# Five experts' rows of x gathered as quarter rows and turned by VectorE in 32x32 blocks instead of by TensorE

## The chip, the cores and the metric

One core of one Trainium2 chip runs one program. Its engines are TensorE (PE in the profile, its weight loads PEld), VectorE (DVE), ScalarE (ACT), GpSimd (POOL) and SyncE (SP), which work from queues of their own, in order, and wait for each other by semaphores. The metric is the device time of one execution in microseconds (us); lower is better.

## The reference

Attention over 8 batches of 448 tokens with 12 heads of 64, then a mixture of 8 experts over the 3584 rows of its output. The routing is greedy: all 3584 x 8 logits are sorted, and a token goes to its best expert that still has room, 448 rows each.

```python
x = attention(q, k, v, cap)                 # [3584, 768]; scores are cap * tanh(scores / cap)
logits = x @ w_gate                         # [3584, 8]
for idx in np.argsort(-logits.flatten()):   # greedy, 448 rows to an expert
    ...
for e in range(8):
    mask = assigned == e
    h = np.maximum(x[mask] @ w1[e], 0.0)    # w1[e] is [768, 1024]
    out[mask] = h @ w2[e]                   # w2[e] is [1024, 768]
```

## The kernel before

**Stages.** Attention takes the first 340 us or so and leaves x in DRAM (`xs`, one row of 768 floats to a token). Then the routing's first round runs, and from about 390 us `ffn_all` goes through the experts in the order in which the routing fills them, p = 0 to 7. All products are made to nearly full fp32 precision out of two halves: every operand is split into a high part (ScalarE copies it to fp32r: `xgh`, `w1h`, `w2h`) and the rest (`xgl`, `w1l`, `w2l`: the operand minus its high part). VectorE makes the rests of x, GpSimd those of the weights (line 723, called by `split1` and `split2`).

**One expert.** `ffn1` makes h in 8 blocks f of 128 columns, each of 18 matmuls (6 chunks c of the 768 inputs, three products each): 144 matmuls. `ffn2` makes the output in 8 units u (two column halves, four tiles of rows), 24 or 16 matmuls each: 176. Every matmul calls `tick`, and these 320 ticks per expert are the clock by which everything else is put between them when the program is written: engines marked for manual scheduling (TensorE, ScalarE, VectorE, GpSimd) run in exactly the order written.

**x of the next expert.** When the routing has the row numbers of expert p+1, `tick` calls `gather` (line 746): four indirect DMAs from GpSimd's queue fetch 128, 128, 128 and 64 rows of 3 KB into the one buffer `xg`, token on the partition. In units u = 5, 6 and 7 of `ffn2` of expert p, `xtr` (line 762) turns chunk after chunk: four TensorE transpositions into a PSUM tile `psX`, a ScalarE copy to `xgh` (line 767) and a VectorE subtraction to `xgl` (line 768). The list `CP` says after which matmul of which unit a chunk comes: one in u = 5, three in u = 6, two in u = 7. The first layer's weights are loaded so that chunk c holds input rows 128c to 128c+127 (line 707).

**The routing.** `phases0` is a generator that `tick` resumes; each `yield n` says after how many ticks it goes on, a negative number at which tick of all. For p = 1 to 7 it proposes each token's best expert, searches the threshold in three selects of four steps each (on VectorE five compares, line 484, and a step that reads a TensorE sum, lines 488 to 496), and takes the winner (`best`, with `qq` of line 559 and `sx` of line 548 on VectorE). Then `finalise` makes the row numbers: VectorE writes two masks and a running count (lines 573 to 577); 12 ticks later TensorE sums the counts over partitions (line 584); VectorE makes positions and two one-hot tables (lines 588 to 602); 18 ticks later TensorE multiplies them (line 606); and after two more small steps `idx` is there (line 617). The winner of p is searched while expert p-1 is computed. The line `yield -((p-1)*320+145)` holds `finalise` back until tick 145 of expert p-1, which is the second matmul of its `ffn2`. Counted in ticks of expert p-1, the search for p ends at 101 (p = 3), 100 (p = 4, 5, 6); the last expert needs none.

**GpSimd's queue** in an expert: 14 or so splits of weights, one about every nine ticks through `ffn1`, with a one-element memset between two (`gap`), the last at tick 137 (w2's second half, piece 3); then the gather; then in `ffn2` four scattered writes of the expert before (line 804) and the first two splits for the next expert.

Of the kernel before, what the change touches and what calls it, by code (L numbers as in the profile page):

```python
# [6 lines left out]
F32=mybir.dt.float32; F32R=mybir.dt.float32r; BF16=mybir.dt.bfloat16; F16=mybir.dt.float16; I32=mybir.dt.int32; I16=mybir.dt.int16  # L7
AF=mybir.ActivationFunctionType; ALU=mybir.AluOpType; AX=mybir.AxisListType
# [9 lines left out]
def attention(nc, tc, c1, xp, pM, q, k, v, cap, w_gate, xs, L1, ident, on_logits, on_turn, NDEF, xd, setup):  # L18
# [3 lines left out]
    B,H,S,D=q.shape  # L22
    CP=112; NJ=S//CP; NP=H//2; NQ=NP//2; E=w_gate.shape[1]; HG=2
    N=B*NQ
    xT={}; rin={}; xn={}; spilled={}; todo=list(range(B-NDEF,B-2))
    def xt(b,p,late=None):
# [5 lines left out]
        if p==0:  # L32
            alt=late and (b in spilled and (b-B)%2 or b==B-1)
            xn[b]=(late[1] if alt else xp).tile([CP,NJ,H,D],F32,name="xn",bufs=1)
        ps=late[0].tile([128,512],F32,name="psL") if late else pM.tile([128,512],F32,name="psM")
        for j in range(NJ):
            nc.tensor.transpose(ps[:CP,j*128:(j+1)*128],xT[b][:,p,j*CP:(j+1)*CP],ident)  # L37
        def rest():
            src=ps[:CP,:].rearrange("p (j h d) -> p j h d",j=NJ,h=2)
            if late:  # L40
                raw=late[1].tile([CP,512],F32,name="raw")
                nc.scalar.activation(raw,ps[:CP,:],AF.Copy)  # L42
                src=raw.rearrange("p (j h d) -> p j h d",j=NJ,h=2)
# [264 lines left out]
ACF=1  # L308
LF=1
TA=0  # L310
EW=1; WT=4; PB=lambda nc: nc.gpsimd
FMAX=3.4028234e38
class Routing:
    def __init__(s, nc, cp, NT, E):
# [3 lines left out]
    def setup(s):  # L318
        nc=s.nc; cp=s.cp; E=s.E; NT=s.NT
        CP=112; NC=s.NC  # L320
        t=lambda n,sh,dt=F32: cp.tile(sh,dt,name="r_"+n)
# [39 lines left out]
        nc.vector.tensor_scalar(qi,qi,4,None,op0=ALU.arith_shift_right)  # L361
        s.qm=t("qm",[128,32])
        nc.gpsimd.tensor_scalar(s.qm,qi,8.0,None,op0=ALU.is_equal)
        kv=t("kv",[128,3])
        nc.gpsimd.iota(kv,[[1,3]],base=1,channel_multiplier=0,allow_small_or_imprecise_dtypes=True)
        G=16*(NC//16)*112
# [3 lines left out]
        for n,base,f in (("A",1.0,2.0),("B",-2048.0,2.0**-12),("C",1024.0,2.0**-22)):  # L370
            S=s.steps[n]
            T0=s.T0[n]=t("T0"+n,[128,3]); H=s.H[n]=t("H"+n,[128,S,6]); C=s.C[n]=t("C"+n,[128,S,3])
            x=float(4**(S-1))
# [128 lines left out]
    def search(s,wp,turned=()):  # L502
# [66 lines left out]
    def finalise(s,wp,L,update):  # L569
        nc=s.nc; T=s.T; NC=s.NC; v=nc.vector  # L570
# [11 lines left out]
        ps=s.psum()  # L582
# [21 lines left out]
        ps=s.psum()  # L604
# [7 lines left out]
        ps=s.psum()  # L612
        s.selmm=nc.tensor.matmul(ps[:,:28],s.sel,ev,start=True,stop=True)
        v.scalar_tensor_tensor(s.ixf[:,:28],ps[:,:28],float(s.NT//2),s.qm[:,:28],op0=ALU.add,op1=ALU.mult)
        idx=wp.tile([128,4],I32,name="idx",bufs=8)
        with nc.allow_low_precision(reason="one term of each sum is not zero"):
            mark=v.tensor_reduce(idx,s.ixf.rearrange("p (t r) -> p t r",r=8),axis=AX.X,op=ALU.add)
        s.results.append((idx,s.ei))
        yield 1
        if update:  # L620
          with s.tc.issue_after(mark.ins) if s.cur==0 else nullcontext():
            z=wp.tile([112,1],F32,name="zz")
# [15 lines left out]
    def phases0(s,wp,L,turned):  # L638
        HA=[7,10]; HB=3
        for p in range(s.E):  # L640
            s.hA=HA[min(p,len(HA))-1] if p else 7; s.hB=HB; s.na=2 if p<9 else 1
            s.cur=p
            if p:
                s.propose(L,0,s.NC)
                yield 30
            yield from (s.search(wp,turned if p==0 else ()) if p<s.E-1 else s.last(wp))
            yield -((p-1)*320+145) if p>1 else 4
            yield from s.finalise(wp,L,p<s.E-1)


# [1 line left out]
def ffn_all(nc, tc, ctx, rt, xs, w1, w2, out, ident, E, wp, deferred, xctx, gen):  # L652
    C=448; DM=768; DC=6; DF=1024; FC=8; HD=384
# [3 lines left out]
    res=rt.results  # L657
# [34 lines left out]
    f2=ctx.enter_context(tc.tile_pool(name="f2",bufs=1))  # L692
# [9 lines left out]
    def load1(p,i,gate=None):  # L702
        if p>=E: return
        e=expert(p)
        t=ws.tile([128,DC,128],F32,name="w1r",bufs=W1B)
        if gate is not None: nc.gpsimd.tensor_copy(t[0:1,0,0:1],gate)
        nc.sync.dma_start(t,w1[bass.ds(e,1),:,i*128:i*128+128].rearrange("o (c p) f -> p (o c) f",p=128))
        raw[p,1,i]=t
    def load2(p,i,gate=None):
        if p>=E: return  # L710
# [21 lines left out]
        view=use=lambda t:t.rearrange("p (o d) -> p o d",o=2)  # L732
        cut((p,2,hf,i),src,[128,2*HD],"w2",8,None,view,use)
    xgs={}; xgT={}
    CP=[[int(y) for y in x] for x in ',,,,,0,123,45'.split(',')]
    CL=[[[]]*6+[[None,0,1],[2,3]],[[]]*6+[[0,1,2],[3,4]]]
    def newx(p):
        if p not in xgT: xgT[p]=(fp.tile([128,DC,C],F32R,name="xgh"),fp.tile([128,DC,C],F32R,name="xgl"))
# [2 lines left out]
    def gather(p):  # L741
        if p>=E or p in xgs: return
        need(p)
        t=xgs[p]=xgp
        for j,(o,n) in enumerate(TS):
            g=nc.gpsimd.indirect_dma_start(out=t[:n,j*DM:(j+1)*DM],out_offset=None,in_=xs,in_offset=bass.IndirectOffsetOnAxis(ap=res[p][0][:n,j:j+1],axis=0))
        return g
    def tx(p,n):
        newx(p)
        w=rt.psum()  # L750
        ps=[(ph.tile([128,512],F32,name="psH") if c>1 else pt.tile([128,512],F32,name="psX")) for c in range(n)]
        for j,(o,_) in enumerate(TS):
            for c in range(n): nc.tensor.transpose(ps[c][:,o:o+128],xgs[p][:,j*DM+c*128:j*DM+c*128+128],ident)
            if j<len(TS)-1: warm(WJ,w)
        for c in range(n): cutx(p,c,ps[c])
    def xtr(p,c):
        if p>=E or c is None: return
        newx(p)
        gather(p)
        ps=pt.tile([128,512],F32,name="psX")  # L760
        for j,(o,n) in enumerate(TS):
            nc.tensor.transpose(ps[:,o:o+128],xgs[p][:,j*DM+c*128:j*DM+c*128+128],ident)  # L762
        cutx(p,c,ps)
    def cutx(p,c,ps):
        h,l=xgT[p]
# [44 lines left out]
    def ffn2(p,t,hf,cs,work={}):  # L810
        if p not in ons: ons[p]=(f2.tile([128,3*DM],F32,name="on"),f2.tile([64,DM],F32,name="on3"))
        ps=ph.tile([128,512],F32,name="psH")
        h=hh[p]
        o,n=TS[t]
        terms=((o,0),(512+o,0),(o,1)) if t<3 else ((o,0),(o,1))
        m=0; nm=FC*len(terms)
        for f in range(FC):
            for a,w in terms:
                nc.tensor.matmul(ps[:,:HD],h[:,f,a:a+128],spl[p,2,hf,f//2][w][:,f%2,:],start=(m==0),stop=(m==nm-1))  # L819
                m+=1  # L820
                tick()
                if m%8==4 and m//8<len(cs): xtr(p+1,cs[m//8])
                for z in work.get(m,()): z()
        cols=slice(hf*HD,hf*HD+HD)
        if t<3: nc.scalar.activation(ons[p][0][:,t*DM+hf*HD:t*DM+hf*HD+HD],ps[:,:HD],AF.Copy)  # L825
        else:
            y=f2.tile([64,HD],F32,name="y3",bufs=2)
            nc.scalar.activation(y,ps[64:128,:HD],AF.Copy)
            nc.vector.tensor_tensor(ons[p][1][:,cols],ps[:64,:HD],y,op=ALU.add)
# [17 lines left out]
    for p in range(E):  # L847
        lastp=p==E-1; cur[0]=p
        for f in range(FC):
            if f==0: load2(p,2)  # L850
            if f+W1B-1<FC and (p==0 or f+W1B-1>=W1B): load1(p,f+W1B-1) if (p,1,f+W1B-1) not in raw else None
            if f==2: load2(p,3)
            work={}
            if f+2<FC and (p,1,f+2) not in spl: work[3]=[lambda: split1(p,f+2)]
            at={0:[(11,0,0)],1:[(11,0,1)],2:[(11,0,2)],3:[(11,1,0)],4:[(11,0,3)],5:[(11,1,1)],6:[(11,1,2)],7:[(11,1,3)]}
            if p==0: at={1:[(11,0,0)],2:[(11,0,1)],3:[(11,0,2)],4:[(11,0,3)],5:[(11,1,0)],6:[(3,1,1),(11,1,2)],7:[(3,1,3)]}
            for n,hf,i in at.get(f,()): work[n]=[lambda hf=hf,i=i: split2(p,hf,i)]
            if p==1 and f==0: work[1]=[lambda: xtr(1,5)]
# [12 lines left out]
        for u in range(8):  # L871
            if u==4: load1(p+1,0); load1(p+1,1)
            if u==5: load1(p+1,2); load2(p+1,0)
            if u==6: load1(p+1,3)
            if u==7: load2(p+1,1)
            wk={5:{14:[lambda: split1(p+1,0)]},6:{8:[lambda: split1(p+1,1)]}}.get(u,{})
            if p<1 and u==7: wk={15:[lambda: xtr(p+1,4+p)]}
            ffn2(p,u%4,u//4,(CL[p] if p<1 else CP)[u],wk)
            if u>3: pend.append((p,u%4))


# [58 lines left out]
```

## Time and profile before

| | us |
|---|---|
| median of 3 runs | 919.64 |
| lowest, highest | 918.25, 920.63 |
| the profiled execution | 920.52 |
| its span, first to last instruction | 918.8 |
| experts' stage in the trace | from about 390 to 911 |
| one expert's `ffn1` and `ffn2`, p = 4 | 657.1 to 687.9 and 687.9 to 723.1 |

The profile gives for each engine its busy time, groups of instructions by line with count, busy time and mean, and the idle time before them with what ended it. `f32 x8` after shapes is a count. The timeline has one line per instruction: start, length, engine, line, operation, output<-inputs; in square brackets the idle time before it. Matmuls are pipelined, so the step from one start to the next is what a matmul costs, not its length. Row "PE psH L791 x16" of the chain in order of time means sixteen matmuls of the first layer in the time shown.

### The profile page before, as it was taken

What the parts mean: (1) busy time and instruction counts of PE and PEld (TensorE: products, weight loads), DVE (VectorE), ACT (ScalarE), POOL (GpSimd) and SP (SyncE); (2) the same over time, 40 slices, a digit from 0 to 9 for tenths busy, and PEclk for the clock granted to TensorE, in tenths of its full rate; (3) what the DMA queues carried; (4) which work ended last, traced back from release to release, by engine and by line L of the source; (5) the groups of instructions that cost most, each with busy time, mean ns of one, the idle gap of its engine ahead of it and who ended that gap; (6) DMA issues with size and microseconds to landing.
All of it is one profiled execution on the core that took longest, in us unless ns stands there. A gap on an engine that the chain in (4) does not pass through costs nothing.

```text
span 918.8 us, 17575 instructions
## 1 busy us (share of the span) xinstructions
PE 880.7 (96%) x6318; PEld 640.7 (70%) x6318; DVE 611.0 (67%) x2012; ACT 582.2 (63%) x836; POOL 351.9 (38%) x514
## 2 busy tenths in 40 slices
PE   7899999999999997799999999999999999999996
PEld 4333444444333335688989989989989899999996
DVE  3777988989788688776777776766777764231210
ACT  6999999999999957273482662662752742522520
POOL 7200000000000008583494392492682673754831
PEclk9999999999999999799999999999999999999999
DMA  8799999997993007750914516416406407426201
GB/s 119 115 132 131 137 166 170 134 159 134 192 142 88 1 5 256 233 205 27 322 47 162 196 40 228 137 33 232 147 18 249 147 2 264 131 72 246 78 10 52
DMA packets 291704, 123.09 MB, mean 134 GB/s; under 512 B 224768, under 2 KB 275712, under 8 KB 291104
## 3 DMA queue, kind: packets, MB, share of 16 engines
q1 hardware_dynamic: 285104, 99.70, 48.0%
q0 software_dynamic: 4656, 22.02, 6.4%
q8 instruction: 50, 0.82, 0.4%
q10 hardware_dynamic: 1856, 0.23, 0.2%
q14 instruction: 38, 0.31, 0.1%
HBM read 97.15 MB, written 24.77 MB: 133 GB/s over the span
## 4 chain that ended last, share of the span: by engine, by line
PE 73%; ACT 9%; issue 9%; DVE 4%; POOL 3%; DMA 1%; SPq 0%; POOLq 0%; ACTq 0%; DVEq 0%
PE psH L791 22%; PE psH L819 22%; PE psA L187 10%; PE psS L149 8%; ACT e L155 5%; PE psM L204 3%; ACT e L159 3%; PE psS L154 2%; PE psX L762 2%; DVE cmpD L484 1%; POOL out_dram L804 1%; POOL w1l L723 1%; PE psL L37 1%; POOL w2l L723 1%; PE psM L215 1%
## 5 line engine op out<-in xcount | busy, mean ns | idle before, releaser
L819 PE MATMUL psH<-w2h,hh 128*128 128x384 f32 x896 | 249.0, 343 | 0.0
L819 PE MATMUL psH<-w2l,hh 128*128 128x384 f32 x512 | 174.5, 341 | 0.0
L155 ACT ACTIVATE e<-psS,s 128x896 f32<-128x896 f32 x168 | 160.7, 995 | 19.3 <-PE psS L149 11.4
L819 PEld LDWEIGHTS psH<-w2h,hh 128*128 128x128 f32 x896 | 162.7, 189 | 0.2
L159 ACT ACTIVATE e<-e,bias,capt 128x1792 f32<-128x1792 f32 (+2 forms) x74 | 154.2, 2084 | 2.5
L791 PE MATMUL psH<-xgh,w1h 128*128 128x448 f32 x384 | 142.9, 372 | 0.3 <-ACT xgh L767 0.3
L45 POOL TENSOR_TENSOR xn<-raw,rin 112x512 f32<-112x512 f32 x24 | 24.4, 1049 | 309.9 <-ACT raw L42 308.7
L149 PE MATMUL psS<-tq,tk 64*64 64x448 f32 x1152 | 130.5, 546 | 12.4 <-ACT e L155 12.4
L791 PE MATMUL psH<-xgl,w1h 128*128 128x448 f32 x384 | 141.9, 370 | 0.0
L791 PE MATMUL psH<-xgh,w1l 128*128 128x448 f32 x384 | 141.2, 368 | 0.0
L723 POOL TENSOR_TENSOR w2l<-w2r,w2h 128x768 fp32r<-128x768 f32 x64 | 118.1, 1846 | 11.0 <-ACT w2h L719 10.8
L723 POOL TENSOR_TENSOR w1l<-w1r,w1h 128x768 fp32r<-128x768 f32 x62 | 114.3, 1843 | 20.7 <-ACT w1h L719 16.8
L187 PE MATMUL psA<-e,nv 64*64 64x448 f32 x1104 | 122.0, 547 | 0.2 <-ACT e L159 0.2
L825 ACT ACTIVATE on<-psH 128x384 f32<-128x384 f32 x48 | 23.6, 492 | 127.3 <-PE psH L819 122.1
L163 DVE TENSOR_TENSOR es<-es,e 64x896 f32<-64x896 f32 (+2 forms) x74 | 100.5, 1359 | 4.8 <-ACT e L159 3.5
L799 DVE SCALAR_TENSOR_TENSOR hh<-psH,hh 128x64 fp32r<-128x64 f32 (+1 forms) x128 | 44.0, 386 | 85.2 <-ACT hh L797 84.6
L149 PEld LDWEIGHTS psS<-tq,tk 64*64 64x64 f32 x1152 | 41.9, 132 | 80.7 <-ACT e L155 45.7
L819 PEld LDWEIGHTS psH<-w2l,hh 128*128 128x128 f32 x512 | 96.6, 189 | 0.0
L187 PEld LDWEIGHTS psA<-e,nv 64*64 64x64 f32 x1104 | 44.8, 134 | 62.1 <-issue 50.5
L797 ACT ACTIVATE hh<-psH 128x448 fp32r<-128x448 f32 x64 | 34.7, 542 | 70.5 <-PE psH L791 66.3
L791 PEld LDWEIGHTS psH<-xgh,w1h 128*128 128x128 f32 x384 | 72.5, 189 | 6.1 <-ACT xgh L767 0.5
L791 PEld LDWEIGHTS psH<-xgh,w1l 128*128 128x128 f32 x384 | 72.3, 188 | 5.6
(317 smaller groups left out, 1305.3 us busy)
## 6 DMA issues: line engine op xcount, KB each, us to landing
w1r<-in_moe_w_dram SPq DMA_DIRECT2D x64, 384.0 KB, 4.2
w2r<-in_moe_w_dram SPq DMA_DIRECT2D x32, 768.0 KB, 7.8
k<-in_k_dram SPq DMA_DIRECT2D x92, 112.0 KB, 3.3
q<-in_q_dram SPq DMA_DIRECT2D x92, 112.0 KB, 3.9
nv<-in_v_dram SPq DMA_DIRECT2D x72, 128.0 KB, 3.9
xs<-xn SPq DMA_DIRECT2D x4, 1344.0 KB, 7.6
xs<-xn SPq DMA_DIRECT2D x4, 896.0 KB
xd<-xT SPq DMA_DIRECT2D x2, 1344.0 KB
```

The lines of the kernel that those rows point to most:

```text
L45: (nc.gpsimd if late else nc.vector).tensor_tensor(xn[b][:,:,h0:h0+3:2,:],src, rin[b][:,:,2*p:2*p+2].unsqueeze(3).broadcast_to([CP,NJ,2,D] ...
L149: for c in range(2): nc.tensor.matmul(ps[c*64:c*64+64,h,:S],tks[g,0][hp,o,u*128+c*64:u*128+c*64+64],tks[g,1][hp,o,:],start=True,stop=True)
L155: nc.scalar.activation(ev(g,r),ps[:,:,:S],AF.Tanh,scale=s1)
L159: nc.scalar.activation(e,e,AF.Exp,scale=capt,bias=bias)
L163: t=es_t[g]; add=lambda o,a,b: nc.vector.tensor_tensor(o,a,b,op=ALU.add)
L187: nc.tensor.matmul(avp[g,o][h*64:h*64+64,:S],lhs,rhs[hp,h,:],start=(j==0 and x==0),stop=(j==3 and (g<N-1 or o==0)))
L204: nc.tensor.matmul(ps[g*32:g*32+32,:S],lhs,rhs,start=first,stop=last)
L723: (eng or nc.gpsimd).tensor_tensor(view(l),r,view(h).bitcast(F32),op=ALU.subtract)
L791: nc.tensor.matmul(ps[:,:C],a[:,c,:],b[:,c,:],start=(m==0),stop=(m==DC*3-1)); m+=1
L797: nc.scalar.activation(h[:,:C],ps[:,:C],AF.Relu)
L799: nc.vector.scalar_tensor_tensor(h[:,d:d+b-a],ps[:,a:b],0.0,h[:,a:b].bitcast(F32),op0=ALU.max,op1=ALU.subtract)
L819: nc.tensor.matmul(ps[:,:HD],h[:,f,a:a+128],spl[p,2,hf,f//2][w][:,f%2,:],start=(m==0),stop=(m==nm-1))
```

## The change

For the experts p = 3 to 7 (`GN=3`):

- `finalise` makes a second table `idg` [128, 14] of row numbers for quarter rows (a 32-partition block b holds quarter b of 32 tokens), with two more VectorE instructions; `setup` makes two constants for it.
- `gather` issues fourteen indirect DMAs of 128 quarter rows (768 bytes each) instead of four of whole rows.
- `turnx` takes the place of the four transpositions: one VectorE transposition of 32x32 blocks per chunk reads every sixth float of `xg` and writes `xt` in SBUF; ScalarE makes `xgh` and VectorE `xgl` from `xt`, the subtraction of a chunk written behind the transposition of the next. Each call puts the routing's next step off by five ticks.
- One chunk moves from u = 5's first place to its third; the other five keep their places.
- `finalise` is held only until tick 90 of expert p-1 (for p = 7 the number is 60, and the six times five ticks bring it to 90).

For all experts the first layer's input rows are taken in another order: chunk c holds rows 6i + c on partition i. So w1 is loaded in that order, and the transpositions that stay with TensorE (p = 0, 1, 2) read every sixth float of `xg` as their weights.

```diff
-EW=1; WT=4; PB=lambda nc: nc.gpsimd
+EW=1; GN=3; WT=4; PB=lambda nc: nc.gpsimd
...
-        s.results.append((idx,s.ei))
+        idg=None
+        if s.cur>=GN:
+            gx=wp.tile([128,28],F32,name="gx",bufs=1)
+            v.scalar_tensor_tensor(gx,ps[:,:28],s.gb,s.gm,op0=ALU.add,op1=ALU.mult)
+            idg=wp.tile([128,14],I32,name="idg",bufs=2)
...
+                v.tensor_reduce(idg,gx.rearrange("p (t r) -> p t r",r=2),axis=AX.X,op=ALU.add)
+        s.results.append((idx,s.ei,idg))
...
-            yield -((p-1)*320+145) if p>1 else 4
+            yield -((p-1)*320+(90 if p<7 else 60)) if p>1 else 4
...
-        nc.sync.dma_start(t,w1[bass.ds(e,1),:,i*128:i*128+128].rearrange("o (c p) f -> p (o c) f",p=128))
+        nc.sync.dma_start(t,w1[bass.ds(e,1),:,i*128:i*128+128].rearrange("o (p c) f -> p (o c) f",c=DC))
...
+    CN=[[[int(y) if y!='-' else None for y in x] for x in z.split(',')] for z in (',,,,,--0,123,45',)*2]
...
+        if p>=GN:
+            for j in range(14):
+                nc.gpsimd.indirect_dma_start(out=t[:,j*192:j*192+192],out_offset=None,in_=xs.rearrange("n (b d) -> (n b) d",b=4),in_offset=bass.IndirectOffsetOnAxis(ap=res[p][2][:,j:j+1],axis=0))
+            return
...
+    def chunk(p,j,c): return xgs[p][:,j*DM:j*DM+DM].rearrange("t (d c) -> t d c",c=DC)[:,:,c]
+    half=[]
+    def turnx(p,c):
+        x=f2.tile([128,C],F32,name="xt",bufs=2)
+        nc.vector.transpose(x.rearrange("p (t i) -> p t i",i=32),xgs[p][:,:14*192].rearrange("p (t d c) -> p t d c",d=32,c=DC)[:,:,:,c])
+        h,l=xgT[p]
+        nc.scalar.activation(h[:,c,:],x,AF.Copy)
+        half.append(lambda: nc.vector.tensor_tensor(l[:,c,:],x,h[:,c,:].bitcast(F32),op=ALU.subtract))
+        cnt[0]-=5
+        while len(half)>(1 if c<DC-1 else 0): half.pop(0)()
...
+        if p>=GN: return turnx(p,c)
...
-            nc.tensor.transpose(ps[:,o:o+128],xgs[p][:,j*DM+c*128:j*DM+c*128+128],ident)
+            nc.tensor.transpose(ps[:,o:o+128],chunk(p,j,c),ident)
...
-            ffn2(p,u%4,u//4,(CL[p] if p<1 else CP)[u],wk)
+            ffn2(p,u%4,u//4,(CL[p] if p<1 else CP if p+1<GN else CN[p>3])[u],wk)
```

**Where instructions move.** TensorE, the counts' sum of `finalise` for p = 5: before, it stands among the second layer's matmuls (`w2h`, `w2l`) of expert 4.

```order
L819 MATMUL psH<-w2l,hh 128x384
L819 MATMUL psH<-w2h,hh 128x384
L584 LDWEIGHTS r_lo
L584 MATMUL psR<-scan,r_lo 112x2
L585 LDWEIGHTS r_up
L585 MATMUL psR<-scan,r_up 112x1
L819 MATMUL psH<-w2h,hh 128x384
```

In the changed kernel it stands among the first layer's (`xgh` or `xgl` with `w1h` or `w1l`), behind matmul 102 of the 144.

```order
L823 MATMUL psH<-xgl,w1h 128x448
L823 MATMUL psH<-xgh,w1l 128x448
L593 LDWEIGHTS r_lo
L593 MATMUL psR<-scan,r_lo 112x2
L594 LDWEIGHTS r_up
L594 MATMUL psR<-scan,r_up 112x1
L823 MATMUL psH<-xgh,w1h 128x448
```

TensorE's sum, and with it everything behind it, now follows VectorE's count 50 matmuls earlier, in `ffn1`. On VectorE the same `finalise` stood behind six `hh` instructions (the last three blocks of h) that separated it from the end of the search; now it follows `sx` directly.

```order
L568 SCALAR_TENSOR_TENSOR qq<-r_K_340,wA,r_K_341 112x32
L552 TENSOR_TENSOR wt<-psR,wm 112x8
L554 TENSOR_REDUCE wB<-wt 112x1
L557 SCALAR_TENSOR_TENSOR sx,e8s<-wt,wB,r_e8c 112x8
L582 TENSOR_SCALAR gt<-qq,wB 112x32
L583 TENSOR_SCALAR gteq<-qq,wB 112x32
L584 SCALAR_TENSOR_TENSOR gteq<-r_kk,e8s,gt 112x32
L586 SCALAR_TENSOR_TENSOR scan<-r_ones_174,gteq 112x64
```

The three `hh` pairs that came between `sx` and `gt` have moved: one behind `scan`, one behind `oi`, one behind `ev`. GpSimd's queue at the gather for p = 5, in the changed kernel:

```order
L739 TENSOR_TENSOR w2l<-w2r,w2h 128x768
L764 DMA xg<-xs,idg 128x192 x14
L737 MEMSET gap 1x1
L739 TENSOR_TENSOR w2l<-w2r,w2h 128x768
L836 DMA out_dram<-on,idx 3584x768
```

The gather of p = 4 to 7 now stands ahead of the last split of the expert's w2, where before it stood behind it; for p = 3 it still stands behind.

More of the change, by code (lines that the diff above doesn't have):

```diff
@@ L363, in setup @@
         nc.gpsimd.tensor_scalar(s.qm,qi,8.0,None,op0=ALU.is_equal)
+        gi=t("gi",[128,28],I32)
+        nc.gpsimd.iota(gi.rearrange("p (t r) -> p t r",r=2),[[0,14],[16,2]],base=0,channel_multiplier=1)
+        s.gb=t("gb",[128,1])
+        gj=t("gj",[128,1],I32)
+        nc.vector.tensor_scalar(gj,gi[:,0:1],5,None,op0=ALU.arith_shift_right)
+        nc.vector.tensor_scalar(gi,gi,4,1,op0=ALU.arith_shift_right,op1=ALU.bitwise_and)
+        nc.gpsimd.tensor_scalar(s.gb,gj,0.25,float(NT//2),op0=ALU.mult,op1=ALU.add)
+        s.gm=t("gm",[128,28])
+        nc.gpsimd.tensor_scalar(s.gm,gi,0.0,4.0,op0=ALU.is_equal,op1=ALU.mult)
         kv=t("kv",[128,3])
@@ L617, in finalise @@
             mark=v.tensor_reduce(idx,s.ixf.rearrange("p (t r) -> p t r",r=8),axis=AX.X,op=ALU.add)
-        s.results.append((idx,s.ei))
+        idg=None
[3 more added lines that the diff above has]
+            idg=wp.tile([128,14],I32,name="idg",bufs=2)
+            with nc.allow_low_precision(reason="one term of each sum is not zero"):
+                v.tensor_reduce(idg,gx.rearrange("p (t r) -> p t r",r=2),axis=AX.X,op=ALU.add)
+        s.results.append((idx,s.ei,idg))
         yield 1
@@ L734, in ffn_all @@
     xgs={}; xgT={}
-    CP=[[int(y) for y in x] for x in ',,,,,0,123,45'.split(',')]
+    CP=[[int(y) if y!='-' else None for y in x] for x in ',,,,,0,123,45'.split(',')]
+    CN=[[[int(y) if y!='-' else None for y in x] for x in z.split(',')] for z in (',,,,,--0,123,45',)*2]
     CL=[[[]]*6+[[None,0,1],[2,3]],[[]]*6+[[0,1,2],[3,4]]]
@@ L752, in tx @@
         for j,(o,_) in enumerate(TS):
-            for c in range(n): nc.tensor.transpose(ps[c][:,o:o+128],xgs[p][:,j*DM+c*128:j*DM+c*128+128],ident)
+            for c in range(n): nc.tensor.transpose(ps[c][:,o:o+128],chunk(p,j,c),ident)
             if j<len(TS)-1: warm(WJ,w)
```

## The prediction

> **What bounds the kernel now.** I read the page's first and fourth parts first: busy shares, and the chain of waits that ended last, by engine.
>
> ```profile
> PE 880.7 (96%) x6318; PEld 640.7 (70%) x6318; DVE 611.0 (67%) x2012; ACT 582.2 (63%) x836; POOL 351.9 (38%) x514
> PE 73%; ACT 9%; issue 9%; DVE 4%; POOL 3%; DMA 1%; SPq 0%; POOLq 0%; ACTq 0%; DVEq 0%
> ```
>
> TensorE is the end of the chain for nearly three quarters of the span. The shares are averages over attention and experts, so I then took the windows of one expert of the later stage, p = 4, `ffn1` and `ffn2` apart (columns: window, length, then busy time of PE, PEld, DVE, ACT, POOL, clock, DMA share, GB/s).
>
> ```profile
> 657.10:687.90 30.80, 30.79 (x155) 27.05 (x155) 23.47 (x104) 20.30 (x42) 26.76 (x29) 1.00 0.14 40
> 687.90:723.10 35.20, 35.20 (x221) 33.47 (x220) 25.92 (x123) 14.27 (x36) 11.32 (x12) 1.00 0.63 225
> ```
>
> TensorE never rests in either: a matmul taken away there is time saved, a wait brought in there is time lost, one for one. And GpSimd, 38% busy on average, is busy 26.76 of 30.80 us (87%) in `ffn1` but 11.32 of 35.20 in `ffn2`. The change moves VectorE's routing work out of the second window into the first.
>
> The chain in order of time gives the ticks.
>
> ```profile
> 660.37 3.34 PE psH L791 x16
> 695.38 7.05 PE psH L819 x40
> ```
>
> A tick of `ffn1` is 3.34/16 = 0.209 us, one of `ffn2` 7.05/40 = 0.176 us.
>
> **The transpositions that go.** The timeline of TensorE in expert 6's last unit, from one chunk to the next:
>
> ```profile
> 842.43 0.60 PE L762 MATMUL psX<-ident,xg 128*128 128x128 f32 x4
> 842.78 0.42 PE L819 MATMUL psH<-w2h,hh 128*128 128x384 f32 x1
> ...
> 844.26 0.60 PE L762 MATMUL psX<-ident,xg 128*128 128x128 f32 x4
> ```
>
> From start to start 1.83 us hold eight matmuls (1.41) and four transpositions: 0.42 us a chunk. Six chunks for five experts, p = 3 to 7, all in `ffn2` where TensorE is full: 30 x 0.42 = **12.6 us saved**. What is late next decides how much stays.
>
> **The transpositions that remain.** Those of p = 1 and 2 and of the first expert read their weights at every sixth float.
>
> ```profile
> L762 PEld LDWEIGHTS psX<-ident,xg 128*128 128x128 f32 x176 | 21.8, 140 | 2.3 <-DVE xgl L768 0.4 <-DMA xg<-xs,idx 0.3
> ```
>
> 176 become 56 under this line (16 others, on line 753, stand at the first expert's start). No row shows TensorE reading at a stride. If the hop is free, 0; if a weight load takes twice its step of 0.42/4 = 0.105 us, 56 x 0.105 = 5.9 us. Nothing excludes either end; I take the middle, **+3**.
>
> **VectorE's turning.** Contiguous and strided rows of VectorE by shape:
>
> ```profile
> L231 DVE TENSOR_REDUCE L<-lt 112x32 f32<-112x384 f32 x7 | 6.0, 864 | 0.2
> L236 DVE TENSOR_REDUCE lt<-lt 112x32 f32<-112x256 f32 x1 | 0.6, 616 | 0.0
> L424 DVE TENSOR_REDUCE r_m<-L 112x32 f32<-112x256 f32 x7 | 2.9, 417 | 0.2
> L135 DVE STREAM_TRANSPOSE tk<-k 128x448 f32<-128x448 f32 x2 | 1.3, 646 | 5.2 <-DMA k<-in_k_dram 5.2
> L768 DVE TENSOR_TENSOR xgl<-psX,xgh 128x448 fp32r<-128x448 f32 x46 | 28.6, 624 | 39.3 <-ACT xgh L767 38.2 <-issue 0.6
> ```
>
> A contiguous turn of 448 floats takes 0.65 us. The two reductions of 256 floats differ by their order in memory, 616 against 417 ns: 0.8 ns more an element, so 0.65 + 448 x 0.0008 = 1.0 us for a strided turn; bounds 0.65 and, by the slope from 256 to 384 floats (248/128 = 1.94 ns), 1.25. The Trainium skill (Vector Engine (DVE) Microarchitecture Reference, "5.2 Measured stream behaviour on trn2") has 1.73 ns per column for a source that hops at every element, about 0.85 us here as an estimate; the slope of the trace is a little worse, no run here shows a strided turn, and the sum goes by the rows.
>
> The six turns come at ticks 276 to 316, so between the first and the next expert's start lie 44 ticks: 7.7 us, and as the first matmuls need only chunk 0, 16 ticks of `ffn1` more (3.3): 11.0 us. In them VectorE has six turns (6.0), six subtractions (6 x 0.6 = 3.7), part of a select (five compares of 0.44 us and a step) and the copy of ScalarE between, 0.5 us: about 12.5 in experts that still search, 1 to 2 us too many; experts 6 and 7 have no such search. For the starts of p = 3, 4, 5: **+4**, bounds 0 and 10 (with the 1.25 of the bound, or if the turn of chunk 0 waits for the last quarter rows).
>
> **`finalise` among GpSimd's splits.** This decides the case. The trace shows what the same kind of VectorE instruction (two inputs in SBUF) does in `ffn1` of expert 5 and 4: first VectorE, then GpSimd at that place, and last the same two lines while GpSimd rests.
>
> ```profile
> 745.01 1.27 DVE L559 SCALAR_TENSOR_TENSOR qq<-r_K,wA,r_K 112x32 f32<-112x32 f32 x1
> 746.59 1.50 DVE L548 SCALAR_TENSOR_TENSOR sx<-wt,wB,r_e8c 112x8 f32<-112x8 f32 x1
> 678.93 5.00 DVE L559 SCALAR_TENSOR_TENSOR qq<-r_K,wA,r_K 112x32 f32<-112x32 f32 x1
> ```
>
> ```profile
> 744.40 1.82 POOL L723 TENSOR_TENSOR w1l<-w1r,w1h 128x768 fp32r<-128x768 f32 x1
> 746.17 0.09 POOL L721 MEMSET gap<- 1x1 f32 x1
> 746.23 1.84 POOL L723 TENSOR_TENSOR w2l<-w2r,w2h 128x768 fp32r<-128x768 f32 x1
> ...
> 683.82 0.09 POOL L721 MEMSET gap<- 1x1 f32 x1
> ```
>
> ```profile
> 429.97 0.24 DVE L559 SCALAR_TENSOR_TENSOR qq<-r_K,wA,r_K 112x32 f32<-112x32 f32 x1
> 430.56 0.23 DVE L548 SCALAR_TENSOR_TENSOR sx<-wt,wB,r_e8c 112x8 f32<-112x8 f32 x1
> ```
>
> `qq`, begun at 745.01, ends with the split at 746.2; `sx`, in the next split, ends with that one; the one begun at 678.93 came through only when GpSimd paused at 683.8. Free, each takes 0.24 us. The Trainium skill (SBUF — State Buffer, "SBUF: two separate sides") says that GpSimd and VectorE share a port pair as an exclusive lock, held for a whole instruction, against a VectorE instruction with two SBUF inputs when GpSimd reads SBUF; these rows agree, and this rule speaks against the change.
>
> In the present place, `ffn2`, `finalise` runs free (p = 5, the first and last of each half):
>
> ```profile
> 689.14 0.23 DVE L573 TENSOR_SCALAR gt<-qq,wB 112x32 f32<-112x32 f32 x1
> 689.72 0.29 DVE L577 TENSOR_TENSOR_SCAN scan<-r_ones,gteq 112x64 f16<-112x64 f16 x1
> 690.31 0.26 DVE L588 SCALAR_TENSOR_TENSOR pG<-scan,psR,gteq 112x32 f32<-112x32 f16 x1 [0.28 <-PE psR L585]
> 692.20 0.42 DVE L602 TENSOR_TENSOR oi<-oh,r_idc 112x512 f16<-112x512 f16 x1
> ```
>
> Free, the first half takes 1.0 us up to TensorE's sum and the second 2.3 up to its one-hot product. The rooms, in `ffn1`'s ticks, are 12 x 0.209 = 2.5 and 18 x 0.209 = 3.8: 1.5 to spare in each. Eight instructions have two SBUF inputs: two in the first half (`gteq` of line 575, `scan`), six in the second (`pG`, `pE`, `pi`, `oj`, `oh`, `oi`). A split begins about every 1.9 us and lasts 1.84, so such an instruction meets one nearly always; a single wait averages half a split, 0.9 us, and a second one in a row a whole one. Two in the first half: about 1 + 1.8 against 1.5 to spare. Six in the second: up to six splits, were they to follow on without end. They don't: TensorE's queue stands at line 584 or 606 as written, no tick follows, and GpSimd has at most two splits more whose inputs are ready, since ScalarE's copies for later ones stand in its queue behind copies of h that wait for TensorE; then VectorE runs free. So TensorE stands for one to two splits an expert, 1.84 to 3.7 us; I take 2.7, for five experts **+13.5**. The lower bound is 0.5 each (a split met at its end), the upper 5 to 6, by the row of 5.00. Queued behind the waiting VectorE instruction are the `hh` pairs of the next block, which `ffn2` wants only later, and behind TensorE's everything.
>
> **Smaller parts.** Fourteen gathers instead of four:
>
> ```profile
> L746 POOL DMA_INDIRECT xg<-xs,idx x32 | 34.2, 1068 | 77.0 <-DVE zz L623 61.1 <-DVE idx L617 8.6 <-issue 7.3
> 762.03 0.98 POOL L746 DMA_INDIRECT xg<-xs,idx  x1 [8.58 <-DVE zz L623]
> 763.31 1.20 POOL L746 DMA_INDIRECT xg<-xs,idx  x1 [0.30 <-issue]
> 685.61 1.84 POOL L723 TENSOR_TENSOR w2l<-w2r,w2h 128x768 fp32r<-128x768 f32 x1 [1.70 <-ACT w2h L719]
> ```
>
> 14 x (1.07 + 0.3) = 19 us of GpSimd instead of 5.5, mostly in `ffn2`, where GpSimd rests 24 of 35 us. The row numbers come at tick 129 to 144 and the first turn at 276: about 25 us, so the last quarter rows land near the turn; a lateness is in the turning's bounds. The expert's last split of w2, which ran at 685.61, now stands behind the gathers for p = 4 to 7 and ends, from tick 129 to 133 on (27 to 28 us), 19 + 1.8 later, 48 to 49 us after the expert's start; the second column half begins at 30.8 + 35.2/2 = 48.4 and comes to that piece about six ticks later, 49.5. I take 0; if that cover is gone, up to 1.5 each. The changed order of w1's rows keeps 512 bytes a packet and is loaded ahead, the two instructions for `idg` are 0.4 us on a waiting path that has room: 0.
>
> **The sum**, against the profiled execution's 920.5: 920.5 - 12.6 + 3 + 4 + 13.5 = 928.4; that execution lies 0.9 above the median of 919.6, so **927.5 us**.
>
> **The rivals.** First, on the other side: `finalise` waits, but in the rooms. What speaks for it: 745.01 and 746.59 show an instruction let in at each boundary, several short ones may go into one gap, and for p = 5 and 6 the search, now ending at ticks 79 and 75 in the written order, leaves 11 and 15 ticks ahead of the hold at 90. Against it: the row of 5.00, and six instructions in a row. Then TensorE loses 0.5 an expert, 2.5, and with strided loads at 0, turning at 1 and the last split of w2 at 2: 920.5 - 12.6 + 5.5 - 0.9 = 912.5. It decides from where the waits of a half stay under 1.5 us. Chance 0.36; its low end, nothing lost at all, is 907.
>
> Second, the terms cancel: waits of 1.3 an expert (6.5), strided loads and turning at 3 each make 12.5 against 12.6, so 919.5, no change (within 0.3%, 2.8 us, about what a measurement of this kernel can tell). Chance 0.11.
>
> Third, within slower: `finalise` passes only when GpSimd has run dry, 5.0 as in the row of 678.93, five times 25, with 3 and 4: 939; with the strided turn's bound (10) it would be 945. Chance 0.10.
>
> **How the numbers follow.** My forecast has 0.43 and the third rival 0.10: slower 0.53. The first has 0.36, faster; the second 0.11. Both signs hold much, so the range spans them: from the pure gain, 907, to the third rival's 939 with 2 more for a late split, 941. The forecast's own range is 922 to 935.
>
> **What would show it.** In the changed profile: 56 transpositions under TensorE's line instead of 176; TensorE idle in `ffn1` of experts 2 to 6 ahead of the counts' sum and the one-hot product, put down to VectorE, 2 to 4 us an expert, and `finalise`'s two-input instructions 1 to 5 us long there. Strided turns of about 1.0 us, and TensorE waiting for `xgl` at the starts of experts 3 to 5. Weight loads of the transpositions left well above 140 ns. I am wrong if `finalise`'s instructions stay under half a microsecond in `ffn1`, or if they are long and TensorE doesn't stand; then the first rival's time is due. And wrong otherwise if the largest new idle stands at the start of an expert or ahead of a `w2l` matmul.

## The result, and the profile after

The changed kernel takes **958.12 us** in the median of five runs (956.75 to 962.38) against 920.08 for the kernel before (918.25 to 920.63): ratio 1.0425, 95% interval 1.0403 to 1.0447. Forecast were 927.5 us and a range from 907 to 941; the sign was right, the size was not. The profiled execution is the longest of the five, 962.38 us with a span of 960.5, so against the profiled one of before there are 41.7 us of span to explain.

The same parts of the page as before (busy shares; the chain by engine):

```profile
PE 884.7 (92%) x6198; PEld 639.6 (67%) x6198; DVE 671.3 (70%) x2054; ACT 582.6 (61%) x836; POOL 400.1 (42%) x567
PE 57%; issue 13%; DVE 12%; ACT 9%; POOL 5%; DMA 3%; POOLq 0%; DVEq 0%; ACTq 0%
```

TensorE does no less (884.7 us), and its part of the chain has gone from 73 to 57%: it waits. The windows of expert 4, `ffn1`, `ffn2`, and three microseconds of `ffn1` (the columns as in the prediction; the seventh number is the granted clock):

```profile
670.80:713.70 42.90, 35.65 (x161) 30.60 (x160) 33.74 (x119) 21.16 (x42) 26.85 (x31) 0.88 0.42 131
713.70:747.80 34.10, 32.40 (x191) 30.64 (x191) 27.28 (x126) 14.69 (x40) 20.75 (x21) 1.00 0.33 106
702.00:705.00 3.00, 2.86 (x9) 2.58 (x9) 2.83 (x12) 0.12 (x1) 0.00 (x0) 0.50 0.18 56
```

`ffn2` is 1.1 us shorter than before (35.2), `ffn1` 12.1 longer (30.8). Of the 12.1, TensorE idles 7.25 (42.90 less 35.65), and is busy 4.9 longer for nearly the same instructions, at a mean clock of 0.88, down to 0.50 in the third row. The view of what TensorE waited for, four rows of `ffn1` and `ffn2`:

```profile
PE psR L593 <- DVE ei L588: 23.8, 6, 5.7
PE psH L823 <- DVE xgl L776: 3.9, 5, 1.2
PE psH L851 <- DVE hh L831: 2.7, 2, 1.5
PE psH L851 <- DVE wA L571: 1.2, 1, 1.2
```

The first is the counts' sum, 1.6 us in one wait before (the first expert's), now 22.3 us more in five. What VectorE did meanwhile, in experts 4, 5 and 6, from its timeline, and GpSimd beside the first:

```profile
692.59 8.17 DVE L568 SCALAR_TENSOR_TENSOR qq<-r_K,wA,r_K 112x32 f32<-112x32 f32 x1
767.74 9.33 DVE L568 SCALAR_TENSOR_TENSOR qq<-r_K,wA,r_K 112x32 f32<-112x32 f32 x1
837.41 9.18 DVE L582 TENSOR_SCALAR gt<-qq,wB 112x32 f32<-112x32 f32 x1
```

```profile
693.40 0.09 POOL L737 MEMSET gap<- 1x1 f32 x1
...
695.23 0.09 POOL L737 MEMSET gap<- 1x1 f32 x1
695.28 1.85 POOL L739 TENSOR_TENSOR w2l<-w2r,w2h 128x768 fp32r<-128x768 f32 x1
697.07 0.09 POOL L737 MEMSET gap<- 1x1 f32 x1
697.12 1.79 POOL L739 TENSOR_TENSOR w1l<-w1r,w1h 128x768 fp32r<-128x768 f32 x1
698.86 0.09 POOL L737 MEMSET gap<- 1x1 f32 x1
698.91 1.79 POOL L739 TENSOR_TENSOR w2l<-w2r,w2h 128x768 fp32r<-128x768 f32 x1
700.65 0.09 POOL L737 MEMSET gap<- 1x1 f32 x1
706.24 1.83 POOL L739 TENSOR_TENSOR w2l<-w2r,w2h 128x768 fp32r<-128x768 f32 x1 [5.50 <-ACT w2h L735]
```

One instruction waits past four boundaries between splits (693.40 to 698.86), and ends at 700.76, behind the fifth, when GpSimd has run out of ready splits: the next one waits 5.5 us for ScalarE's copy. It is not an instruction of `finalise` that waits, as the prediction had it, but `qq` just ahead of it (for p = 7, which has no search, `gt`, `finalise`'s first); the rest of the chain then runs free. TensorE's side of the same moment:

```profile
702.14 0.16 PE L593 MATMUL psR<-scan,r_lo 112*112 112x2 f16 x1 [4.88 <-DVE ei L588]
702.26 0.72 PE L823 MATMUL psH<-xgh,w1h 128*128 128x448 f32 x1
702.77 0.57 PE L823 MATMUL psH<-xgl,w1h 128*128 128x448 f32 x1
703.15 0.57 PE L823 MATMUL psH<-xgh,w1l 128*128 128x448 f32 x1
```

It stood 4.88 us, and the next matmuls start 0.37 us apart, where a tick had 0.209. In the chain in order of time, the 18 matmuls behind each of the five sums:

```profile
556.41 5.31 PE psH L823 x18
626.33 6.53 PE psH L823 x18
702.39 6.08 PE psH L823 x18
778.71 5.51 PE psH L823 x18
847.52 5.27 PE psH L823 x18
```

At 0.209 us they would take 3.76 each: 28.7 less 18.8 is **9.9 us** lost to the low clock, behind stands of 2.2 to 5.7 us.

### The profile page after: what moved, and what is told of

Read it like the earlier page. It is cut to its first block, busy times and chain, and to the rows that moved or that the text cites. A ratio compares the mean times of both kernels' runs of the same rounds, so it can differ in the third digit from the quotient of the medians.

```text
span 960.5 us, 17436 instructions
## 1 busy us (share of the span) xinstructions
PE 884.7 (92%) x6198; PEld 639.6 (67%) x6198; DVE 671.3 (70%) x2054; ACT 582.6 (61%) x836; POOL 400.1 (42%) x567
## 4 chain that ended last, share of the span: by engine, by line
PE 57%; issue 13%; DVE 12%; ACT 9%; POOL 5%; DMA 3%; POOLq 0%; DVEq 0%; ACTq 0%
PE psH L823 17%; PE psH L851 13%; PE psA L187 9%; PE psS L149 8%; ACT e L155 5%; PE psM L204 3%; ACT e L159 3%; DMA xg<-xs,idx 3%; DVE cmpD L493 2%; PE psS L154 2%; DVE xt L773 2%; POOL xg L764 1%; DVE xgl L776 1%; DVE gt L582 1%; POOL xg L767 1%
## 5 line engine op out<-in xcount | busy, mean ns | idle before, releaser
L851 PE MATMUL psH<-w2h,hh 128*128 128x384 f32 x896 | 244.5, 340 | 3.9 <-DVE hh L831 2.7
L155 ACT ACTIVATE e<-psS,s 128x896 f32<-128x896 f32 x168 | 160.7, 995 | 19.2 <-PE psS L149 11.3
L823 PE MATMUL psH<-xgl,w1h 128*128 128x448 f32 x384 | 147.1, 384 | 4.0 <-DVE xgl L776 3.9
L823 PE MATMUL psH<-xgh,w1h 128*128 128x448 f32 x384 | 148.4, 387 | 0.2 <-ACT xgh L799 0.2
L823 PE MATMUL psH<-xgh,w1l 128*128 128x448 f32 x384 | 145.9, 380 | 0.0
L764 POOL DMA_INDIRECT xg<-xs,idg x70 | 68.9, 984 | 39.3 <-issue 19.8
L823 PEld LDWEIGHTS psH<-xgl,w1h 128*128 128x128 f32 x384 | 75.8, 197 | 12.2 <-DVE xgl L776 6.7
```

The costliest lines, as they stand in the source:

```text
L155: nc.scalar.activation(ev(g,r),ps[:,:,:S],AF.Tanh,scale=s1)
L764: nc.gpsimd.indirect_dma_start(out=t[:,j*192:j*192+192],out_offset=None,in_=xs.rearrange("n (b d) -> (n b) d",b=4),in_offset=bass.Indirect ...
L823: nc.tensor.matmul(ps[:,:C],a[:,c,:],b[:,c,:],start=(m==0),stop=(m==DC*3-1)); m+=1
```

## The experiments

Each is compared with the kernel before as run beside it (medians of 918.6 to 921.9 us). Line numbers shift by a few between kernels.

**The hold alone**, on the kernel before:

```diff
-            yield -((p-1)*320+145) if p>1 else 4
+            yield -((p-1)*320+90) if p>1 else 4
```

The line acts on p = 2 as well, here as in the changed kernel, but the sum of p = 2 stays where it was (at 492.0 us before, 492.4 here).

> The kernel before with one number changed: finalise held to tick 90 of the expert before (145), for all experts; whole-row gathers and TensorE transpositions stay, nothing of VectorE's turning. Theory (the early finalise alone makes the loss: its VectorE chain waits out GpSimd's ready splits, TensorE stands about 4.5 us at the counts' sum in six experts, then runs some 4.5 us at half clock): 6 x (4.5 + 2) = about 39 us, less where VectorE is let in at a boundary, so 945 to 960 us. Rival (VectorE is late because the turning has put it behind, and the splits only lengthen that): no stand at the sum, 918 to 925 us.

968.96 us in a single run, and once more:

> The kernel before with finalise held to tick 90 instead of 145 and nothing else, timed in rounds, since other kernels of the same first call were disturbed in their one look. Theory (the hold alone makes more than the whole loss, with the waits of qq of 12 to 15 us that its first look showed): 955 to 969 us. Rival (that look was disturbed, the hold alone costs little): 920 to 930.

973.31 us (ratio 1.0575, 1.0551 to 1.0598); both lie above what was expected. With nothing of the gathers or the turning, the early `finalise` costs more than the whole change. Here the search ends ten ticks behind the hold, and two `qq` wait 14.9 us, past eight boundaries, until GpSimd has no split ready:

```profile
L559 DVE SCALAR_TENSOR_TENSOR qq<-r_K,wA,r_K x4: 2745/13513/14923, 547.5 to 766.2; 112x32 f32<-112x32 f32 x4
```

(Shortest, median and longest in ns.) And what TensorE waited for:

```profile
PE psH L791 <- DVE hh L799: 14.2, 2, 7.1
PE psR L584 <- DVE ei L579: 13.8, 4, 5.7
```

TensorE stands at the sum, or, where the `hh` pairs queue behind `qq`, for want of a free PSUM tile.

**The changed kernel without five splits an expert**, those between ticks 60 and 110 of experts 2 to 7; the low halves of these weights are left out:

```diff
+        if not eng and cur[0]>=2 and 60<now[0]-320*cur[0]<110:
+            spl[key]=(use(h),use(h)); return
```

> The changed kernel without GpSimd's five splits between ticks 60 and 110 of experts 2 to 7: the low halves of those weights are left out (the high half is used in their place, so TensorE does the same number of products). VectorE's instructions, their order and the hold at 90 are as in the changed kernel. Theory (the splits alone hold VectorE): qq, sx and gt take 0.24 us, no stand at the sum, no fall of the clock there, 958 - 32 = about 926 us, with the waits at the starts of experts 3 to 5 left. Rival (VectorE is behind anyway): the stand at the sum stays above 2 us and the time above 945.

963.89 us in a single run, yet without the stand at the sum; this run had other waits, in the gathers' time. It was run again:

> The kernel without GpSimd's five splits between ticks 60 and 110 once more, timed in rounds. Its first look had no stand at the counts' sum (1.5 us in all), yet 963.9 us: VectorE and ScalarE waited 3 to 6 us at a time for TensorE's semaphore while the fourteen gathers ran, 8 us an expert in ffn2, ending about 2.4 us after the last gather's issue. Theory (these waits belong to the gathers, which the changed kernel hides because VectorE is behind then): again 960 to 966 us, with the same waits at the same places. Rival (a disturbance of that one run): 924 to 932 us and no such waits.

926.95 us (924.8 to 928.91 in four runs), near the 926 of the first theory, and the waits of the first run were gone. `qq` took 0.24 us:

```profile
L568 DVE SCALAR_TENSOR_TENSOR qq<-r_K,wA,r_K x3: 241/244/298, 613.0 to 748.6; 112x32 f32<-112x32 f32 x3
```

What TensorE waited for:

```profile
PE psR L593 <- DVE ei L588: 1.6, 1, 1.6
PE psH L825 <- DVE xgl L778: 3.8, 5, 1.2
PE psH L853 <- DVE hh L833: 2.4, 2, 1.2
```

The five splits an expert thus make some 30 us of the 38; without them the change still loses 8.4 us against the kernel before beside it (918.55).

**The time of the stand filled with work**, on the changed kernel: products of the identity ahead of the counts' sum, 20 (p = 3) and 44.

```diff
         yield 12
         ps=s.psum()
+        if s.cur>=GN: s.fill(20 if s.cur==3 else 44,ps[:,128:256])
...
```

> The changed kernel with small TensorE products of the identity ahead of the counts' sum, 20 for p = 3 and 44 for p = 4 to 7, about 2 and 4.6 us of work in the time in which TensorE stood. They write a part of the sum's PSUM tile that nothing reads. Theory (the clock falls to half because TensorE stood): VectorE's wait stays, the 18 matmuls behind the sum take about 3.8 us instead of 5.3 to 6.5, and the time is 8 to 10 us shorter, about 949 us. Rival (the clock falls for another reason, the gather's traffic or the load of all engines at once): the matmuls behind the sum stay at 5 to 6.5 us and the time at 956 to 962.

1007.77 us in a single run. I had taken a product for as long as a transposition; it takes twice that, so 44 of them 9.8 us, and TensorE was busy far beyond the end of VectorE's wait. Once more, 1003.84 us:

> The changed kernel with products of the identity ahead of the counts' sum (20 for p = 3, 44 for p = 4 to 7) once more, timed in rounds; its first look showed in ffn2 the disturbed waits that were gone when the kernel without the five splits was run again. Theory (the clock falls because TensorE stands): 958 - 8 to 10 = 948 to 950 us, the 18 matmuls behind the sum in about 3.8 us. Rival (the clock falls for another reason, or the filling costs as much as it saves): 956 to 965.

and beside the changed kernel, where the waits in the gathers' time were absent, 970.18 against 955.73:

> The kernel with products of the identity ahead of the counts' sum a third time, beside the changed kernel on one chip, since both looks of it so far were on chips that showed waits during the gathers. Theory (the clock falls because TensorE stands): 8 to 10 us below the changed kernel of the same chip, and 18 matmuls behind the sum in 3.8 us instead of 5.3 to 6.5. Rival (the products take the time in which VectorE would have ended anyway, so what the clock saves the filling costs): within 4 us of it.

Neither theory can be read from such times, but the trace of the third shows the clock at 1.00 behind four of its sums, and 3.75 us for the 18 matmuls there. With half the products:

> The changed kernel with half as many products of the identity ahead of the counts' sum (10 for p = 3, 22 for p = 4 to 7). The run before showed that 44 take 9.8 us, not 4.6, so these take 2.2 and 4.9 us, the length of the stand. Theory (the clock falls because TensorE stands): the 18 matmuls behind the sum take 3.7 us instead of 5.3 to 6.5 and the time is 8 to 10 us below the changed kernel's 956 to 958, about 948 us, although TensorE still gets the counts no earlier. Rival (the clock falls for another reason): 956 to 959.

950.12 us (949.82 to 950.95). In the chain, at the place of expert 4:

```profile
691.01 4.91 PE psR L697 x44
695.98 3.75 PE psH L827 x18
```

The identity's 22 products (two passes each) take the place of the stand, and the 18 matmuls behind take 3.75 us instead of 6.08. The clock falls because TensorE stands; filling the stand is worth 6 to 8 us here (955.73 and 958.12 less 950.12).

**The row order alone**: all eight experts on the old path, with w1's rows in the new order.

```diff
-EW=1; GN=3; WT=4; PB=lambda nc: nc.gpsimd
+EW=1; GN=8; WT=4; PB=lambda nc: nc.gpsimd
-            yield -((p-1)*320+(90 if p<7 else 60)) if p>1 else 4
+            yield -((p-1)*320+145) if p>1 else 4
```

> The changed kernel with all eight experts on the old path (whole-row gathers, TensorE transpositions, finalise held to 145); what is left of the change is the other order of w1's rows and with it the transpositions that read every sixth float. Theory (a strided weight load costs TensorE about 0.05 us more, from the 0.52 against 0.42 to 0.44 us for a chunk in the changed kernel): 48 chunks x 0.09 = 4 us, so 923 to 925 us, with weight loads of about 225 ns against 140. Rival (the row order of w1 costs in its loads, or the strided loads cost nothing): weight loads of 140 ns and 919 to 921 us, or a wait of ScalarE for w1r and more than 930.

927.15 us against 921.9, a single run of each, and 2 us above the theory. The group of weight loads that had 140 ns has:

```profile
L794 PEld LDWEIGHTS psX<-ident,xg 128*128 128x128 f32 x176 | 29.4, 225 | 1.3 <-DMA xg<-xs,idx 0.9 <-DVE xgl L800 0.3
```

48 chunks cost 5.2 us by these two runs, or 0.11 a chunk; in the trace one chunk with the eight matmuls behind it takes 1.92 to 1.94 us where it took 1.84, 0.08 to 0.10 more. That is a fifth to a quarter of 0.42, not the double.

**The hold at other ticks**, in the changed kernel: 145 (written 115 for p = 7) and 116 (86).

> The changed kernel with finalise held to tick 145 again (115 for p = 7, which its six turns bring to 145); gathers, turning and row order stay. Theory (stand and half clock at the sum come from the early place alone, but 14 gathers take 18 us and then land after the turning should begin): no stand at the sum; row numbers at tick 184, the last gather lands some 7 us after tick 276, TensorE waits 3 to 6 us for xgl at each of five experts' starts, with the fall of the clock after it 4 to 8: 918 - 12.6 + 4 + 25 to 40 = 937 to 952 us. Rival (the loss is in turning and gathers wherever finalise stands): 955 or more.

949.91 us. No stand at the sum, and the row numbers too late: VectorE waits 3.8 to 11 us for the last quarter rows of three experts, and then TensorE for VectorE, chunk by chunk (start of expert 4):

```profile
664.11 0.47 PE L823 MATMUL psH<-xgl,w1h 128*128 128x448 f32 x1 [1.08 <-DVE xgl L776]
665.65 0.47 PE L823 MATMUL psH<-xgl,w1h 128*128 128x448 f32 x1 [0.67 <-DVE xgl L776]
667.43 0.74 PE L823 MATMUL psH<-xgl,w1h 128*128 128x448 f32 x1 [0.91 <-DVE xgl L776]
670.79 0.74 PE L823 MATMUL psH<-xgl,w1h 128*128 128x448 f32 x1 [1.33 <-DVE xgl L776]
```

> The changed kernel with finalise held to tick 116 (86 for p = 7): behind the fourth-last split, where GpSimd's queue runs dry by itself, and the gathers behind all splits of the expert. Theory: qq passes before TensorE needs it, so no stand at the sum; the gathers end near tick 280, so little waiting at the turns; what stays is strided weight loads (4) and late turning at the starts of experts 3 to 5 (up to 12) against 12.6 saved: 918 to 928 us. Rival (the gathers hold back the search on VectorE wherever they stand): 940 or more, with waits of fl for TensorE in ffn2.

945.51 us: the theory missed, and the time lies in the rival's range; whether for the rival's reason is not shown. Most experts' stand at the sum is gone, but p = 7 still stands 5.0 us, `pE` and `oi` meet the last splits (1.05 us for TensorE at each product), and at each start `xgl` and the search's step come 0.7 to 2.2 us late. No tick serves both ends: TensorE is kept waiting at the sum or at the start.

**Two experts only**, p = 6 and 7, beside whose turning there is no search; rows in the new order for these alone.

```diff
-EW=1; GN=3; WT=4; PB=lambda nc: nc.gpsimd
+EW=1; GN=6; WT=4; PB=lambda nc: nc.gpsimd
...
-            yield -((p-1)*320+(90 if p<7 else 60)) if p>1 else 4
+            yield -((p-1)*320+(145,125,95)[max(p-5,0)]) if p>1 else 4
...
```

> A version built from what the runs showed: only p = 6 and 7, in whose turning VectorE has no search to do, take the quarter rows and VectorE's turning; the row order of w1 is changed for these two alone, so the other experts' transpositions read contiguous floats; finalise is held to tick 125 for p = 6 and 7 (written 95 for p = 7) and to 145 for the others. Theory (cost lies in the early finalise, the strided loads and the turning beside a search; all three are gone): 2 x 2.6 = 5.2 us saved, up to 2 lost at the late gather and at the sum: 914 to 918 us. Rival (the finalise of p = 6 and 7 still meets splits at tick 125, 5 us and a slow clock each): 922 to 930.

929.54 us (ratio 1.0094, 1.0072 to 1.0116): the rival's range, and 12 us above the theory's. `gt` of p = 7 still waited 7.2 us at tick 125, TensorE 3.2 at the sum, and this run again had waits in the gathers' time: `ffn2` of expert 6 took 39.1 us, 8.6 more than in the changed kernel. It doesn't beat the kernel before.

**A longer pause between splits.**

```diff
-    gap=f2.tile([1,1],F32,name="gap")
+    gap=f2.tile([128,256],F32,name="gap")
```

> The changed kernel with the memset between two splits on GpSimd made 256 elements of 128 partitions long instead of one element, about 0.3 us instead of 0.09. Theory A (a waiting VectorE instruction needs a longer time in which GpSimd reads nothing): qq and gt get in at the first or second boundary, 1 to 3 us instead of 2.7 to 9.3, and the stand at the sum shrinks by some 2 us in five experts: 940 to 952 us. Theory B (VectorE gets in only when GpSimd has nothing ready at all): waits as long as before or longer by the longer memsets, 14 x 0.25 = 3.5 us more work for GpSimd an expert, 958 to 975 us.

973.77 us, theory B. With a memset of 0.30 us between splits, in which GpSimd reads nothing, `qq` of expert 4 waits 11.2 us, past five of them, and the wait for the sum grows from 23.8 to 36.3 us in all.

**The changed kernel beside these:**

> The changed kernel itself once more, on the chip of the two kernels beside it. On two of the chips used so far kernels with fourteen gathers showed 3 to 6 us waits for TensorE's semaphore while the gathers ran, on another they did not; the changed kernel has only been seen without. If those waits belong to the chip, it is 956 to 962 us on a chip without them and 965 to 995 on one with them.

955.73 us (953.15 to 960.53), on the chip on which the kernel without splits and the filled one had first shown waits in the gathers' time. It had none, so they don't belong to that chip.

## Why the prediction failed

**Right as sized.** 12.6 us saved: `ffn2` of experts 5 and 6, with no search beside the turning, went from 34.0 to 32.0 and 30.5 us, 5.5 together where 12 chunks of 0.42 make 5.0. The strided turn was forecast at 1.0 us from two reductions. Its subtraction takes 0.57 to 0.60 us where it runs alone, the 0.6 taken; the mean is higher because those that meet a split take up to 2.5:

```profile
L773 DVE STREAM_TRANSPOSE xt<-xg 128x448 f32<-128x448 f32 x30 | 31.3, 1053 | 2.8 <-DMA xg<-xs,idg 2.3
L776 DVE TENSOR_TENSOR xgl<-xt,xgh 128x448 fp32r<-128x448 f32 x30 | 26.7, 891 | 4.0 <-ACT xgh L775 3.3
```

The strided loads were forecast at +3 for 56 transpositions, 14 chunks: at 0.11 us a chunk they make 1.5, and 2 with the first expert's four chunks, which the forecast left out.

**The step that failed: "So TensorE stands for one to two splits an expert, 1.84 to 3.7 us; I take 2.7, for five experts +13.5."** It measured 22.3, and 9.9 more of which the sum had nothing. Three parts of it were wrong.

First, a wait was taken to end with the running split, and the next instruction to wait anew. The rows of 745.01 and 746.59 showed that; the row of 678.93 showed the other thing, two boundaries passed over until the ready splits were done, and I gave it to a rival with a chance of 0.10, whose 25 us for five stands is close to the 22.3 measured. In the changed kernel the four longest waits, of `qq` in experts 3 to 5 and of `gt` in expert 6 (5.70 to 9.33 us), all ended when GpSimd had nothing ready, and the long pause changes nothing of it. The Trainium skill (SBUF — State Buffer, "SBUF: two separate sides") has the lock held for an instruction. The trace has VectorE kept out by a row of ready ones.

Second, the place. I costed `finalise` and its eight instructions; `qq` and `sx` ahead of it, quoted in the prediction as evidence, were not in the sum, though the hold had given them 45 ticks of cover before and gives 11 to 15 or none now. By the prediction's own sign, `finalise`'s instructions had to be 1 to 5 us long; but for `gt` of p = 7 they took 0.63 us at most, and yet the time of the first rival did not come, since the wait had moved to `qq`. That GpSimd has some two splits left once TensorE stands was right (697.12, just begun, and 698.91: 3.5 us). But the free chain behind the wait, from `wt` to the count, 1.45 us, comes on top, and the two make the 4.9 of expert 4.

Third, nothing was put down for what a stand does to TensorE afterwards. The half clock of the matmuls behind it costs 1.5 to 2.8 us each time in this trace. The prediction's own view has the granted clock in every window; all were 1.00, and TensorE never stood in them. The Trainium skill (TensorE: Matmul & The Clock Gate, "Part 1: The HAM clock gate") says that the clock goes to half after an idle window of about 3.4 us and comes back after as long a busy one. Here the clock was low behind each of the stands of 4.5 to 5.7 us, and behind one of 2.21 us it had a mean of 0.71; in the repeated run of the changed kernel the same stand of 2.21 us left it at 1.00, so a stand of that length does not always cost it (the windows behind the sum for p = 3, first and repeated run):

```profile
556.20:562.00 5.80, 5.80 (x25) 5.09 (x25) 3.38 (x12) 1.27 (x2) 1.39 (x1) 0.71 0.62 177
551.70:557.50 5.80, 5.80 (x32) 5.08 (x31) 4.11 (x14) 1.28 (x2) 1.84 (x1) 1.00 0.62 170
```

**The turning was undersized.** Forecast +4 (0 to 10) for the starts of p = 3 to 5. With the splits out of the way, the windows of `ffn1` of experts 3, 4 and 5 are

```profile
590.40:624.90 34.50, 32.12 (x163) 27.18 (x162) 28.07 (x124) 21.29 (x42) 17.76 (x20) 1.00 0.45 139
658.40:695.10 36.70, 34.42 (x162) 29.61 (x161) 26.02 (x120) 21.15 (x42) 17.90 (x21) 0.91 0.50 156
728.80:762.80 34.00, 32.37 (x162) 27.20 (x161) 25.07 (x112) 19.95 (x38) 17.87 (x21) 1.00 0.53 167
```

against 30.84, 30.84 and 30.74 before: 12.8 us more. The sum asked how late VectorE would be in all; TensorE asks for a chunk every 3 x 0.209 = 0.63 us, and a chunk takes VectorE 1.55 us (turn and subtraction), so each late chunk is a stand of its own. In expert 4 three of these stands, 0.48, 1.20 and 0.59 us within 3.5 us, were followed by half the clock as well, about 2.4 us of its window:

```profile
663.90:669.50 5.60, 5.54 (x16) 4.62 (x16) 3.49 (x16) 4.56 (x9) 4.09 (x5) 0.50 0.16 35
```

About 1.2 us of each of these windows is at their end, where the routing's next step stands ahead of the last `hh` on VectorE. So some 9 us lie at the starts, just inside the forecast's bound of 10 and far from its +4.

**Not forecast at all: 4 us behind the end.** From the start of the last write's issue to the end of the span it is 7.2 us before, 11.2 after, and 8.8 with two experts:

```profile
911.58 0.97 POOL L804 DMA_INDIRECT out_dram<-on,ih  x1 [3.11 <-ACT on L825]
```

```profile
949.26 0.97 POOL L836 DMA_INDIRECT out_dram<-on,ih  x1 [3.10 <-ACT on L857]
```

```profile
922.53 0.97 POOL L837 DMA_INDIRECT out_dram<-on,ih  x1 [3.11 <-ACT on L858]
```

(Spans 918.8, 960.5 and 931.3.) The changed kernel issues 50 gathers more, the one with two experts 20: 0.08 us each, paid when the program ends. All four traces of kernels with whole-row gathers alone have 7.2 us there, all eleven with five experts on quarter rows 11.2 to 11.3. The prediction had looked for their price only where they run.

**The books.** Of 41.7 us of span: 1.1 before the experts, 4.0 behind them; of the 36.6 between, 22.3 stand at the sum, 9.9 low clock behind it, and 4.4 what is left of late starts and strided loads against the saving.

**Still open.** Why the kernels with fourteen gathers showed in some runs, not in others, waits of VectorE and ScalarE for TensorE in the gathers' time (963.89 against 926.95 us for one kernel; 1003.84 against 970.18 for another). And why some boundaries between splits let a waiting VectorE instruction in, five in the kernel before and one in the changed one, and the others, three in the one before and 18 in the changed one, don't.

## What to carry to other kernels

Before moving a step on VectorE, look at what GpSimd has queued at its new place: an instruction that waits for GpSimd, as `qq` did, may wait for all that is ready there, not only for what runs. Price a stand of TensorE with the slow matmuls behind it, and take into the sum every instruction that loses its cover by the move, those ahead of the moved step too. A supply in pieces is judged piece by piece against the rate at which it is used up.

## What the runs showed of the hardware

- A VectorE instruction waited up to 14.9 us for a row of GpSimd instructions of 1.8 us, in another kernel 11.2 us past pauses of 0.3 us in which GpSimd only writes; `gt`, which reads one tensor from SBUF beside a column of scalars, waited as `qq` with two.
- Behind stands of 4.5 to 5.7 us TensorE ran at half clock for 3 to 5.5 us (twice the 1.5 to 2.8 lost); behind one of 2.21 us it did so in one run and not in another; three short stands close together (0.48, 1.20, 0.59 us) were enough once. With products of no use in the stand it stayed at full.
- A TensorE weight load at every sixth float took 225 ns against 140, and a chunk of four such transpositions about 0.1 us more.
- Each added indirect DMA lengthened the span behind the start of the last write's issue by 0.08 us (7.2, 8.8 and 11.2 us with 32, 52 and 82 gathers).
